# Score matmuls of both heads of a pair in one alternating group, later chunks spread over the expert slots, and a planner that may keep an engine free

## The chip, the cores and the metric

The kernel runs on one core of a Trainium2 chip. A core has a matmul engine (TensorE, PE in the profile, with its weight loads as PEld), VectorE (DVE), ScalarE (ACT), GpSimd (POOL) and SyncE (SP), which here issues nearly all DMAs. The metric is device microseconds for one execution. An execution of the kernel before takes 314.53 us (median of three runs, 313.73 to 315.22).

## The reference, cut to what matters

Stage one is a linear attention with a decaying state, for 4 batches, 8 heads, 768 steps and head size 48. Stage two sends each of the 3072 rows of its result (384 wide) through four two-layer experts and adds them with row weights.

```python
for t in range(S):                       # per batch and head
    cur = outer(u * k[t], v[t])
    y[t] = r[t] @ (state + cur)
    state = w[:, None] * state + outer(k[t], v[t])
x = y.transpose(0, 2, 1, 3).reshape(3072, 384)
p = domain_probs / (domain_probs.sum(-1) + 1e-9)
for e in range(4):                       # w1: 384 x 1024, w2: 1024 x 384
    out += p[:, e:e+1] * (relu(x @ w1[e]) @ w2[e])
```

## The kernel before, in words

**Tiles.** The 768 steps are cut into 6 pieces of 128 for each of the 4 batches: 24 chunks, `ci` = 0 to 23, batch `ci % 4`, piece `ci // 4`. Four chunks with the same piece form a group of 512 rows, `sc` = 0 to 5, which the experts take at once.

**One chunk of attention.** Three loads bring R, K and V (`Rt`, `Kt`, `Vt`, line 172, 192 KB each). DVE multiplies R and K with powers of the decay (`RK`, line 287; jobs `scale`). `RK` is turned so that the head size lies along partitions (`RKT`): for chunks 0 to 9 by PE transposes (line 337) and a copy, from chunk 10 on by a DMA transpose that SP issues (line 326). Two heads share the 128 partitions: the first of each pair has rows 0 to 63, the second rows 64 to 127. The score matmuls (`At_ps`, line 357) contract over 64 rows only: four for the first heads (`j` = 0), into one PSUM tile, and four for the second heads (`j` = 1), into another. In the program these are two jobs, `("At", ci, 0)` and `("At", ci, 1)`, that the planner may put apart. DVE masks each tile (`AtM`, line 366); PE multiplies with V and with the old state (`Y_ps`, lines 381 and 388); DVE adds the current step's share (`Ysb`, line 397), for which POOL and DVE make `ruk`, `dcoef` and `dv`. `Ysb` is transposed into the experts' input `xTe` (by PE to chunk 9, by DMA from chunk 10). For the state, PE makes `St_ps` (line 429), DVE adds it to the old state (`Tn`, line 444), and POOL scales it into `S` (line 449), which the same batch's next chunk reads four chunks later.

**The experts.** `SLOTS` lists 24 pairs of an expert `e` and a group `sc`, in the order of their rank. A slot is 8 first-layer groups (`hT_ps`, line 490: 3 matmuls of 512 columns; for three early slots line 484: 12 matmuls of 128 columns, chunk by chunk), each followed by an ACT relu, and 4 second-layer groups (`out_ps`, line 515: 8 matmuls of 384 columns), each followed by an evacuation into `oacc` (line 523 on ACT for expert 0, line 525 on DVE for the others). The weights arrive in 24 pieces (`wst`, lines 180 and 183), and ACT or DVE casts each to bf16 (lines 72 and 74).

**What sets the order.** Every piece of work is a job with a cost per engine, needed jobs, buffers that it takes and a rank. A small event-driven planner (lines 547 to 632) runs at build time: whenever an engine is free, it takes the job of least rank that is ready and whose buffers are free. The sequence it finds is what is issued, engine by engine; on the chip each engine works through its own sequence in that order, and waits only for the data and buffers of the instruction that is next. Attention jobs have ranks below those of most expert jobs, so attention runs as early as its loads allow, and SP's order of loads is `ORDER` (line 191). Where the planner expects PE to idle in the first 30 us, it puts in matmuls on constants (`spin`, line 157).

Of the kernel before, what the change touches and what calls it, by code (L numbers as in the profile page):

```python
# [19 lines left out]
def kernel(  # L20
# [12 lines left out]
    nc = tc.nc  # L33
# [96 lines left out]
    BACKLOG = 6.0  # L130
    SLOTS = [(0, 0, 1), (1, 0, 0), (0, 1, 1), (1, 1, 1), (2, 0, 0), (2, 1, 0), (3, 0, 0), (3, 1, 0)]
# [9 lines left out]
    def job(name, on, run, needs=(), rank=0.0, takes=(), drops=(), moves=None):  # L141
        j = Job()
        j.name, j.on, j.run, j.needs, j.rank = name, on, run, list(needs), rank
# [22 lines left out]
    def load_chunk(ci):  # L166
        b, c = ci % B, ci // B
        sl = slice(c * C, (c + 1) * C)
        for i, (n, src) in enumerate((("Rt", r), ("Kt", k), ("Vt", v))):
            def run(n=n, src=src):  # L170
                t = tl[n, ci] = work.tile([128, H, D], F32, tag=n, bufs=NIN, name=n)
                nc.sync.dma_start(t, src[b, :, sl, :].transpose([1, 0, 2]))
            load_job((n, ci), 1.0, run, (("inp", ci),))

    def load_w(m, e):
        for i, (a, bb) in enumerate(PIECES):
            def run(i=i, a=a, bb=bb):
                t = tl["wst", m, e, i] = work.tile([128, 3 * Dm], F32, tag="wst", bufs=8, name="wst")
                if m == 1:
                    nc.sync.dma_start(t[:, 0:(bb - a) * Dm].rearrange("p (d f) -> p d f", d=NDB),  # L180
                                      w1_v[e][:, :, a * 128:bb * 128])
                else:
                    nc.sync.dma_start(t[:, 0:(bb - a) * Dm].rearrange("p (f d) -> p f d", d=Dm),
                                      w2_v[e][:, a:bb, :])
            load_job(("wst", m, e, i), 0.52 * (bb - a), run, (("wst", m, e, i),))
# [5 lines left out]
    ORDER = ("c0 p w1e0 c1 c2 c3 w2e0 c4 w1e1 w2e1 c5 c6 c7 w1e2 w2e2 c8 w1e3 c9 w2e3 " +  # L191
             " ".join(f"c{i}" for i in range(10, TOTC))).split()
    for what in ORDER:
        if what == "p":
            load_p()
        elif what[0] == "c":
            load_chunk(int(what[1:]))
        else:
            load_w(int(what[1]), int(what[3:]))


    def cast(m, e, i, rank):
# [11 lines left out]
        if e == 0:  # L214
            on = {"A": 0.36 * n}
        job(("cast", m, e, i), on, run, [("wst", m, e, i)], rank, (), (("wst", m, e, i),))
# [51 lines left out]
    job("pn", {"V": 1.1}, c_pn, ["pt"], 5.5, (), (("mm", "pp"),))  # L268
# [7 lines left out]
    def attention(ci):  # L276
# [6 lines left out]
        pre = [("S", ci - NRK), ("T", ci - NRK, 1)] if ci >= NRK else []  # L283

# [46 lines left out]
        else:  # L331
# [21 lines left out]
        def at(j):  # L353
            def run():
                ps = tl["At", ci, j] = psum.tile([128, NP, C], F32, tag="At", bufs=2, name="At_ps")
                for q in range(NP):
                    nc.tensor.matmul(ps[:, q, :], tl["RKT", ci][j * P2:(j + 1) * P2, 1, q, :],  # L357
                                     tl["RKT", ci][j * P2:(j + 1) * P2, 0, q, :],
                                     start=True, stop=True)
            return run  # L360

        def mk(j):
# [316 lines left out]
```

## Time and profile before

| | us |
|---|---|
| median of the timed runs | 314.53 |
| the profiled execution, whole | 316.11 |
| its span in the trace | 314.3 |
| PE busy | 299.6 (95%) |
| DVE busy | 161.6 (51%) |
| ACT busy | 155.2 (49%) |
| POOL busy | 102.3 (33%) |

How to read it: the span runs from the first instruction of the program to its last, and the profiled execution took 1.8 us more than its span. PE's busy time counts each matmul from its start to its modelled end, and matmuls overlap, so a PE that shows as busy can still be waiting for up to the length of a matmul; what a matmul costs in a stream is read from the starts of the ones that follow. The timeline view merges equal instructions that follow one another: start, time from the first start to the last end, line, operation, count, and in brackets the idle time before and what ended it.

### The profile page before, as it was taken

To read this page: it belongs to the slowest core of one execution; us is meant where nothing else is said; L and a number is where in the kernel's file an instruction comes from. 1 tells how busy PE (TensorE), PEld (TensorE's weight loads), DVE (VectorE), ACT (ScalarE), POOL (GpSimd) and SP (SyncE) were. 2 spreads that over 40 slices of the span, in tenths; PEclk is the share of its full clock that TensorE was granted. 3 is DMA by queue.
4 is the path that set the end of the run, shared out by engine and by line. 5 is a ranking of instruction groups with operands and counts; after the bars stand their busy time and mean duration, and the time that the engine had idled before them with its cause. 6 is when DMAs were issued, how large, how long until landed. Compare 5 with 4: busy or idle time off the path is not lost.

```text
span 314.3 us, 5691 instructions
## 1 busy us (share of the span) xinstructions
PE 299.6 (95%) x2232; PEld 172.3 (55%) x2232; DVE 161.6 (51%) x298; ACT 155.2 (49%) x253; POOL 102.3 (33%) x133
## 2 busy tenths in 40 slices
PE   5799999999998999998999999999999999999995
PEld 2476566876554555555555555555555555555553
DVE  5797578988989997697732231022210221201223
ACT  5467867756333333333545345734456444465440
POOL 3375097566999984756400000000000000000000
PEclk9999999999999999999999999999999999999999
DMA  7999999999999995799500031000020000200002
GB/s 166 250 268 259 298 187 366 255 255 215 206 197 174 177 194 117 190 143 200 118 0 1 2 100 52 1 0 0 27 75 0 2 0 2 75 25 0 2 0 100
DMA packets 108110, 36.92 MB, mean 117 GB/s; under 512 B 96282, under 2 KB 108060, under 8 KB 108084
## 3 DMA queue, kind: packets, MB, share of 16 engines
q1 hardware_dynamic: 108068, 36.56, 49.5%
q8 instruction: 17, 0.28, 0.4%
q14 instruction: 9, 0.07, 0.1%
q10 hardware_dynamic: 16, 0.00, 0.0%
HBM read 26.79 MB, written 4.72 MB: 100 GB/s over the span
## 4 chain that ended last, share of the span: by engine, by line
PE 65%; DMA 16%; DVE 11%; ACT 2%; issue 2%; SPq 2%; POOL 1%; DVEq 0%; POOLq 0%; ACTq 0%
PE out_ps L515 31%; PE hT_ps L490 29%; DMA wst<-in_moe_w_dram 8%; DVE RK L287 4%; DMA RKT<-RK 3%; DVE AtM L366 3%; DMA Rt<-in_r_dram 2%; DMA Kt<-in_k_dram 2%; PE At_ps L357 2%; PE hT_ps L484 2%; DVE oacc L525 1%; DVE Tn L444 1%; ACT hTs L499 1%; DVE Ysb L397 1%; PE RKT_ps L337 1%
## 5 line engine op out<-in xcount | busy, mean ns | idle before, releaser
L501 ACT ACTIVATE hTs<-hT_ps 128x512 bf16<-128x512 f32 x168 | 99.8, 597 | 113.2 <-PE hT_ps L490 108.8
L515 PE MATMUL out_ps<-w_sb,hTs 128*128 128x384 bf16 x768 | 139.9, 326 | 0.0
L490 PE MATMUL hT_ps<-xTe,w_sb 128*128 128x512 bf16 x504 | 124.3, 379 | 0.0
L525 DVE SCALAR_TENSOR_TENSOR oacc<-out_ps,p_nat,oacc 128x384 f32<-128x384 f32 x72 | 44.3, 616 | 124.1 <-PE out_ps L515 123.9
L515 PEld LDWEIGHTS <-hTs 128*128 128x128 bf16 x768 | 73.9, 98 | 54.9
L490 PEld LDWEIGHTS <-w_sb 128*128 128x128 bf16 x504 | 46.8, 98 | 46.9
L366 DVE TENSOR_TENSOR AtM<-At_ps,mask 128x512 bf16<-128x512 f32 x48 | 32.5, 684 | 3.2 <-PE At_ps L357 2.9
L299 POOL TENSOR_TENSOR ruk<-Rt,Kt 128x384 f32<-128x384 f32 x24 | 25.1, 1050 | 20.9 <-DMA Kt<-in_k_dram 20.8
L303 POOL TENSOR_TENSOR ruk<-ruk,U_sd 128x384 f32<-128x384 f32 x24 | 26.6, 1107 | 1.5 <-ACT U_sd L244 1.0
L319 POOL TENSOR_TENSOR dv<-Vt,dcoef 128x384 f32<-128x384 f32 x24 | 21.2, 885 | 14.4 <-DVE Ysb L397 8.2
L449 POOL TENSOR_TENSOR S<-Tn,wC 64x192 bf16<-64x192 f32 x32 | 18.5, 579 | 13.6 <-DVE Tn L444 12.2
L523 ACT ACTIVATE oacc<-out_ps,p_nat 128x384 f32<-128x384 f32 x24 | 13.9, 580 | 17.7 <-PE out_ps L515 17.7
L357 PE MATMUL At_ps<-RKT 64*128 64x128 bf16 x192 | 18.7, 222 | 2.8 <-DMA RKT<-RK 1.1
L72 ACT CAST w_sb<-wst 128x1152 bf16<-128x1152 f32 (+1 forms) x16 | 16.3, 1032 | 8.1 <-DMA wst<-in_moe_w_dram 8.1
L484 PE MATMUL hT_ps<-xTe,w_sb 128*128 128x128 bf16 x288 | 19.4, 223 | 0.4 <-DVE xTe L74 0.4
L287 DVE TENSOR_TENSOR RK<-Rt,W_sd 128x384 bf16<-128x384 f32 x20 | 17.4, 870 | 2.1 <-DMA Rt<-in_r_dram 2.1
L357 PEld LDWEIGHTS <-RKT 64*128 64x128 bf16 x192 | 10.6, 95 | 14.2 <-issue 7.4
L484 PEld LDWEIGHTS <-w_sb 128*128 128x128 bf16 x288 | 17.1, 100 | 1.4 <-DVE xTe L74 0.5
L287 DVE TENSOR_TENSOR RK<-Kt,W_sd 128x384 bf16<-128x384 f32 x20 | 17.2, 859 | 0.6 <-DMA Kt<-in_k_dram 0.5
L314 DVE TENSOR_REDUCE dcoef<-ruk 128x8 f32<-128x384 f32 x24 | 13.0, 546 | 6.5 <-POOL ruk L303 6.3
L499 ACT ACTIVATE hTs<-hT_ps 128x512 bf16<-128x512 f32 x24 | 13.6, 600 | 3.0 <-PE hT_ps L484 2.8
L397 DVE TENSOR_TENSOR Ysb<-Y_ps,dv 128x384 bf16<-128x384 f32 x24 | 13.2, 549 | 1.3 <-PE Y_ps L388 1.2
(59 smaller groups left out, 134.8 us busy)
## 6 DMA issues: line engine op xcount, KB each, us to landing
wst<-in_moe_w_dram SPq DMA_DIRECT2D x16, 576.0 KB, 5.7
Rt<-in_r_dram SPq DMA_DIRECT2D x24, 192.0 KB, 3.8
Kt<-in_k_dram SPq DMA_DIRECT2D x24, 192.0 KB, 4.0
Vt<-in_v_dram SPq DMA_DIRECT2D x24, 192.0 KB, 3.9
out_dram<-oacc SPq DMA_DIRECT2D x24, 192.0 KB, 2.1
wst<-in_moe_w_dram SPq DMA_DIRECT2D x8, 384.0 KB, 6.4
RKT<-RK SPq DMA_TRANSPOSE x14, 3.8
xTe<-Ysb SPq DMA_TRANSPOSE x14, 2.5
```

Source lines behind the costliest of these rows:

```text
L287: nc.vector.tensor_mul(RK[:, i, :, 0:D], tl[("Kt", "Rt")[1 - i], ci], tl["W", i] if ci < SUB else W_sd[i])
L299: nc.gpsimd.tensor_mul(tl["ruk", ci], tl["Rt", ci], tl["Kt", ci])
L303: lambda: nc.gpsimd.tensor_mul(tl["ruk", ci], tl["ruk", ci], U_sd),
L319: nc.gpsimd.tensor_mul(tl["dv", ci], tl["Vt", ci], tl["dcoef", ci].to_broadcast((128, H, D)))
L357: nc.tensor.matmul(ps[:, q, :], tl["RKT", ci][j * P2:(j + 1) * P2, 1, q, :], tl["RKT", ci][j * P2:(j + 1) * P2, 0, q, :], start=True, stop ...
L366: nc.vector.tensor_mul(tl["AtM", ci][:, j], tl["At", ci, j], mask[:, None, :].to_broadcast((128, NP, C)))
L449: nc.gpsimd.tensor_mul(S_new[pr, :, cl], tl["Tn", ci][pr], wC[pr, :, None].to_broadcast((P2, NP, D)))
L484: nc.tensor.matmul(ps[:, i, :], w1_sb[:, e, db, (fb + i) * 128:(fb + i + 1) * 128], xTe[:, db, s0, :], start=(i == 0 and db == 0), stop=(i ...
L490: nc.tensor.matmul(ps[:, 0:n, :].rearrange("p a b -> p (a b)"), w1_sb[:, e, db, fb * 128:(fb + 1) * 128], xTe[:, db, s0:s0 + n, :].rearran ...
L501: nc.scalar.activation(hTs[:, fb, s0:s0 + n, :], ps[:, 0:n, :], AF.Relu)
L515: nc.tensor.matmul(ps, tl["hTs", e, sc][:, fb, s, :], w2_sb[:, e, fb, :], start=(fb == 0), stop=(fb == NFB - 1))
L525: nc.vector.scalar_tensor_tensor(tl["oacc", ci], in0=tl["o", e, ci], scalar=pe, in1=tl["oacc", ci], op0=ALU.mult, op1=ALU.add)
```

## The change

The change has these parts, all in how jobs are defined and planned; what is computed is the same.

1. The two score jobs of a chunk become one, whose eight matmuls alternate between the first and the second head of each pair. Both masks need that one job.
2. The scale jobs of chunks 8 to 23 need the first first-layer group of the slot that stands `LEAD` = 5 places earlier in `SLOTS` (chunk 12: slot 7). This is a need in the planner; on the chip it shows only in the order of each engine's instructions.
3. A job may stand `behind` another: it may start on its engine as soon as the other has been issued, not only when it has ended (second transpose, second mask).
4. In the first 30 us of the plan, an engine that could start a job is kept free if a job of lower rank will be ready for it within 0.6 of the first job's cost.
5. At the start of the kernel: chunk 1's R and K are loaded between the pieces of expert 0's first weights, the row probabilities after chunk 3; the state of the first four chunks and the normalised probabilities wait until the fourth chunk's output is out; POOL may cast expert 0's second weights.

```diff
+    HURRY = 30.0
+    LEAD = 5
...
-    ORDER = ("c0 p w1e0 c1 c2 c3 w2e0 c4 w1e1 w2e1 c5 c6 c7 w1e2 w2e2 c8 w1e3 c9 w2e3 " +
+    ORDER = ("c0 w1e0.0 R1 K1 w1e0.1 w1e0.2 V1 c2 c3 p w2e0 c4 w1e1 w2e1 c5 c6 c7 w1e2 w2e2 c8 w1e3 c9 w2e3 " +
...
         if e == 0:
             on = {"A": 0.36 * n}
+            if m == 2:
+                on["P"] = 0.45 * n
...
-    job("pn", {"V": 1.1}, c_pn, ["pt"], 5.5, (), (("mm", "pp"),))
+    job("pn", {"V": 1.1}, c_pn, ["pt", ("Yout", SUB - 1)], 3.0, (), (("mm", "pp"),))
...
         pre = [("S", ci - NRK), ("T", ci - NRK, 1)] if ci >= NRK else []
+        if ci >= 2 * SUB:
+
+            e_g, sc_g, one = SLOTS[ci - LEAD]
+            pre.append(("l1", e_g, sc_g, 0, 0))
...
-                    [("scale", ci, i)] + ([("T", ci, 0)] if i else []), on_pe,
-                    (("tr", "T", ci),) if i == 0 else ())
+                    [("scale", ci, i)], on_pe, (("tr", "T", ci),) if i == 0 else (),
+                    behind=(("T", ci, 0),) if i else ())
...
-        def at(j):
-            def run():
-                ps = tl["At", ci, j] = psum.tile([128, NP, C], F32, tag="At", bufs=2, name="At_ps")
-                for q in range(NP):
-                    nc.tensor.matmul(ps[:, q, :], tl["RKT", ci][j * P2:(j + 1) * P2, 1, q, :],
+        def at():
+
+            for j in range(2):
+                tl["At", ci, j] = psum.tile([128, NP, C], F32, tag="At", bufs=2, name="At_ps")
+            for q in range(NP):
+                for j in range(2):
+                    nc.tensor.matmul(tl["At", ci, j][:, q, :],
+                                     tl["RKT", ci][j * P2:(j + 1) * P2, 1, q, :],
                                      tl["RKT", ci][j * P2:(j + 1) * P2, 0, q, :],
                                      start=True, stop=True)
-            return run
...
+        job(("At", ci), {"T": 0.42}, at, [ready], on_pe, (("At", ci, 0), ("At", ci, 1)), (("RKT", ci),))
         for j in range(2):
-            job(("At", ci, j), {"T": 0.23}, at(j), [ready] + ([("At", ci, 0)] if j else []), on_pe,
-                (("At", ci, j),), (("RKT", ci),))
-            job(("mask", ci, j), {"V": 0.61}, mk(j), [("At", ci, j)] + ([("mask", ci, 0)] if j else []),
-                rk - 0.5, (("AtM", ci),) if j == 0 else (), (("At", ci, j),))
+            job(("mask", ci, j), {"V": 0.61}, mk(j), [("At", ci)],
+                rk - 0.5, (("AtM", ci),) if j == 0 else (), (("At", ci, j),),
+                behind=(("mask", ci, 0),) if j else ())
...
-        job(("Sm", ci), {"T": 0.17}, smm, [("Y", ci), "wC"] + ([("S", ci - B)] if c else []), on_pe + 1,
+        job(("Sm", ci), {"T": 0.17}, smm, [("Y", ci), "wC", ("S", ci - B) if c else ("Y", SUB - 1)], on_pe + 1,
...
+    def fits(j):
+        if any(n not in gone for n in j.behind):
+            return False
+        new = [t[0] for t in j.takes if t not in held]
+        return all(free[n] >= new.count(n) for n in new)
...
+        if got is not None and now < HURRY:
+
+            us = got.on[e]
+            for i in soon[e]:
+                if i.name not in gone and i.rank < got.rank and fits(i) and                         now < known[i.name] < now + 0.6 * us:
+                    heapq.heappush(waiting[e], (got.rank, got.no, got))
+                    heapq.heappush(events, (known[i.name], seq, "eng", e))
+                    seq += 1
+                    return False
```

Three places show how the instructions move. The lines of the changed kernel stand 18 to 20 further down: its 377 is line 357 before, 510 is 490, 535 is 515, 305 is 287, 386 is 366, 464 is 444.

PE, the score matmuls of chunk 12. Before, the eight matmuls of `RKT_1562` (left out here after the first of each four):

```order
L388 MATMUL Y_ps_1697<-Vb_1500,AtM_1645 128x48
L357 LDWEIGHTS RKT_1562
L357 MATMUL At_ps_1713<-RKT_1562 128x128
...
L490 LDWEIGHTS w1_sb_70
L490 MATMUL hT_ps_1718<-xTe_720,w1_sb_70 128x512
...
L357 MATMUL At_ps_1726<-RKT_1562 128x128
...
L429 LDWEIGHTS RK2_105
```

and after the change, those of `RKT_1881`:

```order
L510 MATMUL hT_ps_1910<-xTe_734,w1_sb_70 128x512
L377 LDWEIGHTS RKT_1881
L377 MATMUL At_ps_1916<-RKT_1881 128x128
...
L377 MATMUL At_ps_1917<-RKT_1881 128x128
...
L535 LDWEIGHTS hTs_1729
L535 MATMUL out_ps_1927<-w2_sb_71,hTs_1729 128x384
```

Two groups of four with other work between them, each for one PSUM tile, have become one group of eight in which every second matmul is for the other tile and the other half of the rows.

DVE, the masks of chunk 9, the last whose operand PE transposes; `S_0_111` is the state of chunk 8's batch, the casts are of expert 3's second weights. Before:

```order
L397 TENSOR_TENSOR Ysb<-Y_ps,dv 128x384
L74 CAST w_sb<-wst 128x1152
L444 TENSOR_TENSOR Tn<-S_0_111,St_ps 64x192 x2
L314 TENSOR_REDUCE dcoef<-ruk 128x8
L74 CAST w_sb<-wst 128x1152
L74 COPY xTe<-xT_ps 128x3x128
L366 TENSOR_TENSOR AtM<-At_ps,mask 128x512
L287 TENSOR_TENSOR RK_105<-Rt,W_sd 128x8x48
L366 TENSOR_TENSOR AtM<-At_ps,mask 128x512
```

and after:

```order
L417 TENSOR_TENSOR Ysb<-Y_ps,dv 128x384
L74 CAST w_sb<-wst 128x1152
L464 TENSOR_TENSOR Tn<-S_0_111,St_ps 64x192 x2
L74 COPY xTe<-xT_ps 128x3x128
L386 TENSOR_TENSOR AtM<-At_ps,mask 128x512 x2
```

One of the two casts has moved to ACT, and chunk 10's first scale no longer stands between the masks.

DVE, the scales of chunk 11 (`RK3_106`) and its masks. Before:

```order
L287 TENSOR_TENSOR RK3_106<-Rt_1318,W0_sd_127 128x8x48
L525 SCALAR_TENSOR_TENSOR oacc_1035<-out_ps_1438,p_nat_131,oacc_1035 128x384
L397 TENSOR_TENSOR Ysb_1484<-Y_ps_1456,dv_1388 128x384
L314 TENSOR_REDUCE dcoef_1497<-ruk_1434 128x8
L287 TENSOR_TENSOR RK3_106<-Kt_1323,W1_sd_128 128x8x48
...
L366 TENSOR_TENSOR AtM_1645<-At_ps_1626,mask_92 128x512
```

and after:

```order
L464 TENSOR_TENSOR Tn_1714<-S2_0_115,St_ps_1702 64x192 x2
L305 TENSOR_TENSOR RK3_106<-Rt_1330,W0_sd_127 128x8x48
L305 TENSOR_TENSOR RK3_106<-Kt_1340,W1_sd_128 128x8x48
L545 SCALAR_TENSOR_TENSOR oacc_1027<-out_ps_1731,p_nat_131,oacc_1027 128x384
L545 SCALAR_TENSOR_TENSOR oacc_1238<-out_ps_1749,p_nat_131,oacc_1238 128x384
L386 TENSOR_TENSOR AtM_1795<-At_ps_1775,mask_92 128x512
```

The scales now follow directly on the state sum of the chunk before, and only two evacuations stand between them and the masks that need their product; before there were 14 rows of other work. From chunk 10 on this pattern repeats once per slot. On PE, between the state matmuls of one chunk (line 449) and the score matmuls of the next, stand six first-layer groups and two second-layer groups; on SP, one DMA transpose of `RK` per slot, with the loads of a chunk four places later behind it.

More of the change, by code (lines that the diff above doesn't have):

```diff
@@ L139, with job @@
         pass
-    def job(name, on, run, needs=(), rank=0.0, takes=(), drops=(), moves=None):
+    def job(name, on, run, needs=(), rank=0.0, takes=(), drops=(), moves=None,
+            behind=()):
         j = Job()
+        j.behind = behind
         j.name, j.on, j.run, j.needs, j.rank = name, on, run, list(needs), rank
@@ L561 @@
     gone = set()
+    unknown = {n: len(q) for n, q in left.items()}
+    known = {n: 0.0 for n in left}
+    soon = {e: [] for e in avail}
     held = set()
@@ L583, in start @@
             if ready_at[j.name] <= now + 1e-9 and \
-                    all(t in held or free[t[0]] > 0 for t in j.takes) and \
+                    fits(j) and \
                     not (j.moves and e == "S" and dma_free[0] > now + BACKLOG):
@@ L607, in start @@
         heapq.heappush(events, (end, seq + 1, "done", j))
+        for u2 in users.get(j.name, ()):
+            unknown[u2.name] -= 1
+            known[u2.name] = max(known[u2.name], end)
+            if not unknown[u2.name] and end < HURRY + 5:
+                for e2 in u2.on:
+                    soon[e2].append(u2)
         seq += 2
```

45 lines of the change are left out of this document (25 added, 20 removed).

## The prediction

> **What bounds the kernel now.** I read the windows view first, over stretches cut where its character changes (columns: stretch, length, busy us and instructions of PE, its weight loads, DVE, ACT and POOL, granted clock, DMA share, GB/s).
>
> ```profile
> 0.00:30.00 30.00, 23.16 (x234) 15.71 (x235) 22.59 (x60) 18.44 (x29) 14.84 (x24) 1.00 0.92 229
> 30.00:77.00 47.00, 45.11 (x526) 32.43 (x524) 37.44 (x64) 32.62 (x50) 26.50 (x33) 1.00 1.00 269
> 77.00:160.00 83.00, 80.36 (x653) 44.15 (x650) 71.32 (x125) 29.77 (x50) 60.99 (x77) 1.00 0.86 166
> 160.00:311.00 151.00, 150.94 (x829) 80.02 (x826) 29.70 (x50) 74.33 (x125) 0.00 (x0) 1.00 0.07 22
> 311.00:314.30 3.30, 0.00 (x0) 0.00 (x0) 0.60 (x1) 0.00 (x0) 0.00 (x0) 0.84 0.33 119
> ```
>
> Four regimes follow one another. To 30 us everything starts up, PE idles 6.8 us. From 30 to 77 us PE is nearly full, but the DMA engines are full (1.00): work cannot come sooner than its data. From 77 to 160 us DVE (71.3 of 83) and PE share the load and PE idles 2.6 us. From 160 us attention is over and PE alone is busy, without a gap, for 151 us; 3.3 us of evacuation and store end the span. So a microsecond of PE work or PE waiting saved after 77 us is saved at the end; one saved before 77 us counts only if the data were there.
>
> The second view is the PE timeline in the third stretch, for the price of a score group.
>
> ```profile
> 113.66 0.82 PE L490 MATMUL hT_ps<-xTe,w_sb 128*128 128x512 bf16 x3
> 114.32 1.46 PE L515 MATMUL out_ps<-w_sb,hTs 128*128 128x384 bf16 x8
> 115.62 0.33 PE L381 MATMUL Y_ps<-S,RKT 128*128 128x96 bf16 x4
> ...
> 116.14 0.81 PE L490 MATMUL hT_ps<-xTe,w_sb 128*128 128x512 bf16 x3
> 116.88 0.39 PE L357 MATMUL At_ps<-RKT 64*128 64x128 bf16 x4
> 117.20 0.82 PE L490 MATMUL hT_ps<-xTe,w_sb 128*128 128x512 bf16 x3
> ```
>
> From start to start, three matmuls of line 490 take 0.66 us when line 515 follows, and 0.74 when a score group follows: 0.08 is lost on entering. The group itself holds PE for 0.32 us, though its four matmuls step by only (0.39 - 0.22) / 3 = 0.058 us; about 0.09 goes on leaving. One group costs 0.32 + 0.08 = **0.40 us**, a chunk 0.80, and some 0.17 of every 0.40 is the turn into 64-row matmuls and out again.
>
> **The change part by part.** *Pairing (A).* The trace holds one case where both groups of a chunk were queued together, chunk 0:
>
> ```profile
> 9.97 0.62 PE L357 MATMUL At_ps<-RKT 64*128 64x128 bf16 x8 [0.86 <-DVE RKT L74]
> ```
>
> and, of all its score matmuls (duration min/median/max in ns),
>
> ```profile
> L357 PE MATMUL At_ps<-RKT x192: 212/216/311, 10.0 to 159.1; 64*128 64x128 bf16 x192
> ```
>
> Eight in 0.62 us. The array was slow there (0.311 us each, the maximum, against 0.216); even at the fast step of 0.058 eight in sequence would need 7 x 0.058 + 0.31 = 0.72. So the two halves ran side by side. The alternating order of the change makes that the rule: four steps of 0.058, one turn in and out of 0.17, about 0.41 us per chunk in place of 0.80, **0.39 saved**. Chunks 10 to 23 have their score work after 77 us: 14 x 0.39 = **5.5 us**. Lower bound, if nothing runs side by side and one turn is saved: 0.17 a chunk, 2.4 us. Upper bound, 0.45 a chunk (a whole group and some of the turn): 6.3. I take 5.5, by the row of eight.
>
> *PE's idle time after 77 us (B).* Its waits in that stretch (total, times, longest):
>
> ```profile
> PE At_ps L357 <- DMA RKT<-RK: 1.1, 1, 1.1
> PE St_ps L429 <- DVE Tn L444: 0.9, 1, 0.9
> PE At_ps L357 <- DVE AtM L366: 0.3, 1, 0.3
> PE St_ps L429 <- DVE Ysb L397: 0.2, 1, 0.2
> ```
>
> All four are score or state matmuls waiting for a crowded DVE or for its product's transpose. With chunks 10 to 23 paced one per slot (10.4 us of expert work: eight groups of 0.65, four of 1.30), DVE has a fixed load per slot. From the groups of the page (busy us and mean ns of one behind the bar):
>
> ```profile
> L525 DVE SCALAR_TENSOR_TENSOR oacc<-out_ps,p_nat,oacc 128x384 f32<-128x384 f32 x72 | 44.3, 616 | 124.1 <-PE out_ps L515 123.9
> L366 DVE TENSOR_TENSOR AtM<-At_ps,mask 128x512 bf16<-128x512 f32 x48 | 32.5, 684 | 3.2 <-PE At_ps L357 2.9
> L314 DVE TENSOR_REDUCE dcoef<-ruk 128x8 f32<-128x384 f32 x24 | 13.0, 546 | 6.5 <-POOL ruk L303 6.3
> L397 DVE TENSOR_TENSOR Ysb<-Y_ps,dv 128x384 bf16<-128x384 f32 x24 | 13.2, 549 | 1.3 <-PE Y_ps L388 1.2
> L449 POOL TENSOR_TENSOR S<-Tn,wC 64x192 bf16<-64x192 f32 x32 | 18.5, 579 | 13.6 <-DVE Tn L444 12.2 <-POOL S L449 0.3
> ```
>
> Four evacuations 2.46, two masks 1.37, two scales 1.71 (twice the median below), `dcoef` 0.55, `Ysb` 0.55 and a state sum of 0.74 (below) make 7.4 us of some 11; DVE is no longer near its limit. The 2.6 us of idle go, and with each of the four waits up to 0.16 that the modelled end of the last matmul covers (0.216 long, next possible after 0.058): **3.2 us**. Bounds 0 (each returns elsewhere) and 3.2.
>
> *The new wait (C).* The pacing takes away slack: the score group of a chunk now follows its scales closely. In the trace the same chain stands once, spread over PE, DVE, POOL and SP:
>
> ```profile
> 127.85 0.33 PE L429 MATMUL St_ps<-Vb,RK 128*128 128x96 bf16 x4
> 128.02 1.46 PE L515 MATMUL out_ps<-w_sb,hTs 128*128 128x384 bf16 x8
> 128.22 0.74 DVE L444 TENSOR_TENSOR Tn<-S,St_ps 64x192 f32<-64x192 bf16 x2 [0.29 <-PE St_ps L429]
> 128.75 1.28 POOL L449 TENSOR_TENSOR S<-Tn,wC 64x192 bf16<-64x192 f32 x2
> 128.99 0.68 DVE L287 TENSOR_TENSOR RK<-Kt,W_sd 128x384 bf16<-128x384 f32 x1
> 129.70 1.24 SPq L326 DMA_TRANSPOSE RKT<-RK  x1
> ```
>
> State matmuls start at 0; state sum done and scale begun at 1.14; two scales at 0.68 end at 2.50; the transpose is issued at 2.53. If an evacuation (0.62) stands before the state sum, 3.15. The transpose lands 3.1 to 4.9 us after its issue, and a scale takes 0.54 to 1.36 (the views of the tile `RKT` and of line 287):
>
> ```profile
> DMA to landing us min/median/max: 3.1/3.8/4.9
> ```
>
> ```profile
> L287 DVE TENSOR_TENSOR RK<-Rt,W_sd x20: 542/856/1362, 26.5 to 151.1; 128x384 bf16<-128x384 f32 x20
> ```
>
> So the operand is there at 5.6 to 6.3 with the shortest landing, 6.9 with the median one. PE in that time has its state matmuls (127.85 to 128.02, 0.17), six groups of 0.66 and two of 1.30: it asks at 6.7. The slack is 0.4 to 1.1 us, or -0.2. SP's queue before that transpose holds loads four chunks ahead and stores, both long released, and the loads of one chunk per slot (0.59 MB, at the 269 GB/s above 2.2 us of 11) leave the DMA engines mostly idle, so I take the short landing: **0.4 us lost in all**, with 14 x 0.2 = 2.8 as the near bound. If PE does wait, the masks of that chunk and DVE's evacuations behind them start that much later; four PSUM buffers absorb it.
>
> *The front (D).* Load order, deferred states, the planner's held engines, second transposes and masks `behind`, and the pairing of chunks 1 to 9 all act before 77 us. There the work hangs on data: DVE's casts wait for weights, and chunk 9's scale and masks stand behind them.
>
> ```profile
> 65.83 0.95 DVE L74 CAST w_sb<-wst 128x768 bf16<-128x768 f32 x1 [0.73 <-DMA wst<-in_moe_w_dram]
> 66.70 0.68 DVE L366 TENSOR_TENSOR AtM<-At_ps,mask 128x512 bf16<-128x512 f32 x1
> 67.30 1.23 DVE L287 TENSOR_TENSOR RK<-Rt,W_sd 128x384 bf16<-128x384 f32 x1
> ...
> 70.50 0.76 DVE L74 CAST w_sb<-wst 128x1152 bf16<-128x1152 f32 x1 [0.73 <-DMA wst<-in_moe_w_dram]
> ...
> 72.40 0.89 DVE L74 CAST w_sb<-wst 128x1152 bf16<-128x1152 f32 x1
> ...
> 73.84 0.69 DVE L366 TENSOR_TENSOR AtM<-At_ps,mask 128x512 bf16<-128x512 f32 x1
> ...
> 70.51 1.50 PE L484 MATMUL hT_ps<-xTe,w_sb 128*128 128x128 bf16 x24
> 71.85 1.46 PE L515 MATMUL out_ps<-w_sb,hTs 128*128 128x384 bf16 x8
> ...
> 75.50 1.46 PE L515 MATMUL out_ps<-w_sb,hTs 128*128 128x384 bf16 x8
> 76.80 0.33 PE L381 MATMUL Y_ps<-S,RKT 128*128 128x96 bf16 x4
> ```
>
> The bytes and their sequence to this point are the same after the change, so the cast that waited until 70.50 waits until then again, whatever was won before. What moves is one cast of 0.89 to ACT. After the first cast, at 71.2, DVE then has the state sum (0.73), a copy (0.36) and both masks (2 x 0.69), done at 73.7. PE takes chunk 9's product there, with one single-chunk group (half of the 1.34 from 70.51 to 71.85, 0.67) and one second-layer group (1.30) behind it that it had done before that product until now: 75.7 against 76.8. I take **0.8 us** won, between 0 and 1.5, since how soon PE is there is not sure. POOL's two new casts can delay chunk 3's `dv` behind them by a few us at 25 us; that is hidden by the same wait for data, and without it would cost up to 2.
>
> Sum: 5.5 + 3.2 + 0.8 - 0.4 = **9.1 us**. The profiled execution took 316.1 (span 314.3 and 1.8 around it), which gives 307.0; it was 1.6 above the median of the timed runs, so on the median: 314.5 - 9.1 = **305.4 us**.
>
> **The rivals.** *Late operands (slower).* Place: the score group of chunks 10 to 23. With DVE and POOL at the same time the scales take 1.36, and the landing is 4.4: 1.14 + 0.62 + 2.72 + 0.03 + 4.4 = 8.9 against 6.7, 2.2 us late in each of 14 slots, 31 us lost against 9.5 won: 336. It decides from 9.5 / 14 = 0.68 us late per slot, an operand at 7.4. For it: half of the scales took 0.86 or more, and pacing ties every slot to one such chain. Against: those stood beside the long POOL products of other chunks, and landings over 4 us belong to stretches with a full DMA queue. 8%.
>
> *The scale waits out POOL's state update.* By the row at 128.75 that update (0.58 a piece, mean of its group) starts inside every such chain. If a scale had to wait for each piece: 2 x (0.55 + 0.58) = 2.26 in place of 1.36, operand at 7.2, 0.5 late, 14 x 0.5 = 7.0, and the time 312. The row at 128.99 speaks against it: beside that update the scale took 0.68, not 1.13. 7%. The Trainium skill, "SBUF — State Buffer", section "SBUF: two separate sides", states just this rule: a VectorE instruction with two SBUF inputs and a GpSimd instruction take turns on a shared port pair, and the one that comes second waits for the whole of the other. By it the time would be that of this rival; the trace agrees only in the long scales, up to 1.36.
>
> *One turn saved, nothing side by side.* A is 2.4, time 308.5. Against it stands the row of eight. 8%.
>
> *The front passes its gains on.* If data, not its transport, was the limit, 9 x 0.39 = 3.5 of chunks 1 to 9 and the 1.9 us that PE idles from 30 to 77 us come on top: 300 to 302. The DMA share of 1.00 speaks against it. 12%.
>
> *No difference.* The planner's sequence loses at the start what A and B win, over 7 us; the front has 6.8 us of idle to lose in, and it must be lost past the data's own time. 5%.
>
> **How the numbers follow.** Forecast 60% (303.5 to 307.5 with the bounds of C and D); the rivals 8, 7, 8, 12 and 5. No change is within 0.5% or 1.6 us, about what a measurement of this kernel can tell. Faster: 60 + 7 + 8 + 12 = 87%; same 5%; slower 8%. The range from 301.2 to 311.5 leaves out late operands and no difference (13%), half of the port rival and a third of the front's: 2 in 10.
>
> **What would show it.** A: score rows of eight, 0.60 us or less from start to modelled end. B: attention runs to some 250 us, DVE below 75% in every stretch after 80. C: PE's waits for `RKT` by DMA sum to under 1 us; over 9 would make the forecast wrong in sign. D: the same expert work is done on PE at 77 us, within 1.5 us. A score row of eight lasting 0.75, or expert groups 0.2 us longer around it, would refute the pairing.

## The result, and the profile after

The changed kernel takes 305.97 us (median of four runs, 305.80 to 307.27). The kernel before took 314.20 beside it (four runs, 313.73 to 315.22). The ratio is 0.974, 95% interval 0.971 to 0.978: 8.2 us less, where 9.1 less and 305.4 us were forecast. The profiled execution took 306.04 (span 304.3) against 316.11 (span 314.3). Some executions, one of the changed kernel too (307.27 us, mean granted clock 0.994), ran at a lower mean clock, and the ratios leave out the two that stood far above the rest of their kernel, 442.04 of the kernel before and 310.90 of e7.

Its windows, with the same columns as those of before (stretch, length, busy us and instructions of PE, PEld, DVE, ACT, POOL, granted clock, DMA share, GB/s):

```profile
0.00:30.00 30.00, 23.11 (x237) 15.31 (x237) 21.43 (x55) 16.93 (x28) 16.64 (x26) 1.00 0.93 223
30.00:77.00 47.00, 43.91 (x535) 31.76 (x535) 35.45 (x68) 33.69 (x50) 25.45 (x34) 1.00 0.99 272
77.00:160.00 83.00, 83.00 (x567) 44.63 (x565) 46.88 (x84) 38.01 (x64) 39.17 (x52) 1.00 0.56 115
160.00:240.00 80.00, 80.00 (x557) 43.19 (x555) 39.35 (x69) 38.08 (x65) 18.66 (x25) 1.00 0.36 78
240.00:300.80 60.80, 60.80 (x342) 32.46 (x340) 13.60 (x23) 27.94 (x47) 0.00 (x0) 1.00 0.06 22
300.80:304.30 3.50, 0.07 (x1) 0.00 (x0) 0.62 (x1) 0.00 (x0) 0.00 (x0) 1.00 0.31 112
```

From 77 us to its last matmul PE is busy all the time (83.00 of 83, 80.00 of 80, 60.80 of 60.80), and the view of PE's waits is empty there; before, 2.6 us were idle. DVE falls from 71.3 to 46.9 us in the third stretch and carries the rest to 240 us; the last attention matmul ends at 241 us, where some 250 was forecast. Before 77 us PE idles more than before (3.1 us against 1.9 from 30 to 77): the front is as full of waits as it was.

A score group in PE's timeline, paced. `At_ps` is line 377 now, the first layer 510, the second 535:

```profile
157.98 1.46 PE L510 MATMUL hT_ps<-xTe,w_sb 128*128 128x512 bf16 x6
159.37 0.40 PE L377 MATMUL At_ps<-RKT 64*128 64x128 bf16 x8
159.70 1.47 PE L535 MATMUL out_ps<-w_sb,hTs 128*128 128x384 bf16 x8
```

Eight matmuls from start to modelled end take 0.40 us, where four took 0.39. From start to start the group holds PE for 0.33; the six matmuls ahead take 1.39 in place of 6 x 0.216, so entering costs 0.09. A chunk's score work is 0.42 us of PE's time in all. Before, it was 0.80 by the prediction's reading. The starts of single matmuls in the trace of before are finer than that row: entering cost 0.096 there and a group of four held PE for 0.326, which makes 0.84 a chunk.

The transposed operand: the issue for chunk 13 on SP, the PE row that uses it, and from the view of the tile `RKT` (77 to 250 us) the time from issue to landing:

```profile
121.43 1.24 SPq L344 DMA_TRANSPOSE RKT<-RK  x1
```

```profile
125.30 0.40 PE L377 MATMUL At_ps<-RKT 64*128 64x128 bf16 x8
```

```profile
DMA to landing us min/median/max: 3.1/3.1/3.6
```

The operand landed at about 124.5, 0.8 us before PE asked. This slack is 0.24 us for chunk 10, 0.5 to 0.8 for those of chunks 12 to 20 whose landing is on record, 1.7 for chunks 21 and 22 and 3.3 for chunk 23.

### The profile page after: what moved, and what is told of

Read it like the earlier page. It is cut to its first block, busy times and chain, and to the rows that moved or that the text cites. A ratio compares the mean times of both kernels' runs of the same rounds, so it can differ in the third digit from the quotient of the medians.

```text
span 304.3 us, 5693 instructions
## 1 busy us (share of the span) xinstructions
PE 290.9 (96%) x2231; PEld 167.4 (55%) x2231; DVE 157.3 (52%) x296; ACT 154.7 (51%) x253; POOL 99.9 (33%) x135
## 4 chain that ended last, share of the span: by engine, by line
PE 78%; DMA 10%; SPq 5%; DVE 3%; issue 1%; ACT 1%; POOL 0%; DVEq 0%
PE out_ps L535 38%; PE hT_ps L510 34%; DMA wst<-in_moe_w_dram 9%; SPq L178 3%; DMA Kt<-in_k_dram 2%; SPq L187 2%; PE At_ps L377 2%; DVE AtM L386 1%; PE Y_ps L408 1%; PE Y_ps L401 1%; DVE w_sb L74 1%; PE St_ps L449 1%; PE hT_ps L504 1%; ACT w_sb L72 1%; PE RKT_ps L355 0%
## 5 line engine op out<-in xcount | busy, mean ns | idle before, releaser
L510 PEld LDWEIGHTS <-w_sb 128*128 128x128 bf16 x504 | 47.3, 98 | 45.3
L386 DVE TENSOR_TENSOR AtM<-At_ps,mask 128x512 bf16<-128x512 f32 x48 | 31.0, 684 | 25.4 <-PE At_ps L377 25.4
L337 POOL TENSOR_TENSOR dv<-Vt,dcoef 128x384 f32<-128x384 f32 x24 | 20.4, 853 | 16.2 <-DVE Ysb L417 7.8
L321 POOL TENSOR_TENSOR ruk<-ruk,U_sd 128x384 f32<-128x384 f32 x24 | 24.5, 1023 | 2.1 <-ACT U_sd L258 1.0
L72 ACT CAST w_sb<-wst 128x1152 bf16<-128x1152 f32 (+1 forms) x15 | 15.3, 1023 | 13.3 <-DMA wst<-in_moe_w_dram 13.3
L504 PEld LDWEIGHTS <-w_sb 128*128 128x128 bf16 x288 | 17.5, 101 | 3.2 <-issue 1.7
L305 DVE TENSOR_TENSOR RK<-Kt,W_sd 128x384 bf16<-128x384 f32 x20 | 15.1, 753 | 0.4 <-DMA Kt<-in_k_dram 0.3
L305 DVE TENSOR_TENSOR RK<-Rt,W_sd 128x384 bf16<-128x384 f32 x20 | 11.9, 595 | 2.0 <-DMA Rt<-in_r_dram 1.7
L464 DVE TENSOR_TENSOR Tn<-S,St_ps 64x192 f32<-64x192 bf16 x32 | 11.1, 347 | 1.9 <-PE St_ps L449 1.4
L76 POOL CAST Vb<-Vt 128x384 bf16<-128x384 f32 x20 | 10.3, 516 | 2.5 <-PE St_ps L449 2.3
```

The source lines that it names most:

```text
L72: nc.scalar.copy(o, i)
L305: nc.vector.tensor_mul(RK[:, i, :, 0:D], tl[("Kt", "Rt")[1 - i], ci], tl["W", i] if ci < SUB else W_sd[i])
L321: lambda: nc.gpsimd.tensor_mul(tl["ruk", ci], tl["ruk", ci], U_sd),
L337: nc.gpsimd.tensor_mul(tl["dv", ci], tl["Vt", ci], tl["dcoef", ci].to_broadcast((128, H, D)))
L386: nc.vector.tensor_mul(tl["AtM", ci][:, j], tl["At", ci, j], mask[:, None, :].to_broadcast((128, NP, C)))
L504: nc.tensor.matmul(ps[:, i, :], w1_sb[:, e, db, (fb + i) * 128:(fb + i + 1) * 128], xTe[:, db, s0, :], start=(i == 0 and db == 0), stop=(i ...
```

## The experiments

Theory: the sum of the prediction. Pairing (A) takes some 0.4 us a chunk off PE, the pace (B) takes away PE's waits, both after 77 us, where PE sets the end; the front (D) gives little, the new wait (C) almost nothing. Rivals: the parts are worth something else apart; pairing saves a turn only; operands come late. In the notes below, a time is the median of that kernel; the kernel before, run between, had medians of 312.9 to 313.6, so the ratios count.

**e1: pairing alone.**

```diff
-            job(("At", ci, j), {"T": 0.23}, at(j), ...)
+        job(("At", ci), {"T": 0.42}, at, [ready], on_pe, (("At", ci, 0), ("At", ci, 1)), ...)
```

> The kernel before with one edit: the eight score matmuls of a chunk are one job, the two halves in turn, and both masks need that job. Load order, deferred states and the pace stay as they were. Theory (the terms of the prediction add): the score work of a chunk falls from 0.84 to 0.42 us of PE time, 14 chunks after 77 us give 5.7 to 5.9; the waits of PE after 77 us stay near 2.6 us, since DVE is as crowded as before: 308 to 309.5 against 314.2. Rival (the pairing only turns PE work into waiting as long as DVE holds 71 of 83 us from 77 to 160 us): PE waits after 77 us grow by 2 us or more, time 311 or more.

Measured: 315.54 us, ratio 1.006 (1.003 to 1.009). The pairing alone did not make the kernel faster; the rival's numbers came true. PE's waits after 77 us:

```profile
PE At_ps L359 <- DMA RKT<-RK: 4.3, 4, 2.0
PE St_ps L430 <- DVE Ysb L398: 1.1, 2, 0.7
PE out_ps L516 <- DVE oacc L526: 1.0, 1, 1.0
PE hT_ps L491 <- issue: 0.5, 3, 0.2
```

They sum to 6.9 us, 4.4 more than before. The longest, around 126 us, in rows of DVE, SP and PE (times in order):

```profile
118.59 1.33 DVE L287 TENSOR_TENSOR RK<-Kt,W_sd 128x384 bf16<-128x384 f32 x1
...
122.41 0.54 DVE L398 TENSOR_TENSOR Ysb<-Y_ps,dv 128x384 bf16<-128x384 f32 x1
```

```profile
121.63 2.46 SPq L405 DMA_TRANSPOSE xTe<-Ysb  x1
124.18 1.26 SPq L326 DMA_TRANSPOSE RKT<-RK  x1
```

```profile
123.93 1.46 PE L516 MATMUL out_ps<-w_sb,hTs 128*128 128x384 bf16 x8
127.38 0.55 PE L359 MATMUL At_ps<-RKT 64*128 64x128 bf16 x8 [1.98 <-DMA RKT<-RK]
```

The second scale ended at 119.92, but SP issued its transpose at 124.18. Ahead of it in SP's queue stood a transpose of `Ysb`, which DVE finished only at 122.95. So PE stood at the score group until the operand had landed. And the wait had a price of its own, in the windows after it:

```profile
127.00:127.40 0.40, 0.02 (x2) 0.03 (x4) 0.00 (x0) 0.00 (x0) 0.00 (x0) 1.00 0.75 213
127.40:130.80 3.40, 3.18 (x25) 1.79 (x27) 2.62 (x4) 0.60 (x1) 0.83 (x1) 0.51 1.07 211
130.80:131.20 0.40, 0.40 (x7) 0.23 (x5) 0.00 (x0) 0.03 (x1) 0.00 (x0) 0.89 1.17 237
```

For 3.4 us after it the granted clock was 0.51: another 3.4 x 0.49 = 1.7 us. Together 4.4 + 1.7 - 5.9 (14 chunks at 0.42) = 0.2 us more; the two profiled executions differ by 0.6 (316.73 against 316.11). Six of the ten executions, this one among them, have a mean granted clock of 0.995 or less, and a median of 316.1; the four others have 314.0, the kernel before 313.6. So the waits eat what the pairing saves, and most of the loss beyond that goes with the half clock.

**e2: the pace alone.**

```diff
+        if ci >= 2 * SUB:
+            e_g, sc_g, one = SLOTS[ci - 5]
+            pre.append(("l1", e_g, sc_g, 0, 0))
```

> The kernel before with one edit: the scales of chunks 8 to 23 also need the first group of first-layer matmuls of the slot five places earlier. The two halves of a score product stay apart. Theory: PE waits of 2.6 us after 77 us (3.2 with the modelled ends) go and nothing takes their place: 311 to 311.5. Rival (operands come late once attention is paced; with two separate groups there is less expert work between the state matmuls and the scores): waits for RKT of 0.2 us and more a slot, 314 or more.

Measured: 312.76, ratio 0.995 (0.992 to 0.998), 1.5 us less; 2.5 to 3 were expected. No wait of PE is left after 77 us, as expected, so B's gain is there. Part of it is given back earlier: up to 77 us PE idles 10.1 us, against 8.7 in the kernel before. Of the score matmuls, 72 have been done by 77 us (view of the tile `At_ps`), 80 in the kernel before:

```profile
L360 PE MATMUL At_ps<-RKT x72: 216/216/311, 9.7 to 66.1; 64*128 64x128 bf16 x72
```

The gate begins at chunk 8, so one chunk's score work moves past 77 us; that this is why PE idles more before is likely, but not shown. The forecast had put no cost on it.

**e3: pairing and pace, without the front.** Both edits above in the kernel before.

> The kernel before with both edits above, and nothing of the front (load order, deferred states, held engines, the cast on POOL, the masks behind each other). Theory: A and B add, 5.7 and 3.2 less: 305.5 from the median of 314.2 without the front, and the front of the whole change is then worth at most the 0.8 us of the prediction, on either side: 305.3 to 306.8. Rival (the front matters and the parts do not add): 308 or more.

Measured: 305.48, ratio 0.973 (0.970 to 0.975), 8.6 us less, as expected. Against the whole change (0.974, 0.971 to 0.978) no difference can be told: the front's own edits are worth nothing that shows, 0.5 us on the wrong side with about 1.4 either way (the pairing of chunks 1 to 9, which the prediction counts to the front, is in e3 too). The two edits together give 8.6; apart they give -1.9 and 1.5.

**e4: the changed kernel without the pace.**

```diff
-            e_g, sc_g, one = SLOTS[ci - LEAD]
-            pre.append(("l1", e_g, sc_g, 0, 0))
```

> The changed kernel without the pace (the lines that make the scales of chunks 8 to 23 need a slot's first matmuls). Theory: the waits of PE after 77 us come back, 2 to 3 us, the rest stays: 308 to 309 against 306.0, and attention ends before 165 us again. Rival (pairing and the new front had already removed what PE waited for, the pace is worth nothing): 305.7 to 306.7.

Measured: 311.84, ratio 0.995 (0.992 to 0.998); 308 to 309 was expected. Without the pace 6.5 us are lost by the ratios, twice the 3.2 of term B. The window of the crowded stretch, and the waits of PE after 77 us that are over 1 us:

```profile
77.00:160.00 83.00, 77.31 (x654) 43.26 (x663) 68.66 (x126) 32.15 (x54) 60.29 (x77) 1.00 0.84 166
```

```profile
PE At_ps L373 <- DMA RKT<-RK: 2.1, 4, 0.8
PE Y_ps L404 <- DVE AtM L382: 1.8, 4, 0.9
```

All waits sum to 4.8 us. Again PE, with less to do per chunk, waits for attention.

**e5: head after head in one job.**

```diff
-            for q in range(NP):
-                for j in range(2):
+            for j in range(2):
+                for q in range(NP):
```

> The changed kernel with the two loops of the score job exchanged: first the four matmuls of one half, then the four of the other, still one job. Theory (what counts is that both halves are queued together; chunk 0 of the kernel before, written in this order, ran its eight in 0.62 us): as the changed kernel, 305.5 to 306.5, score rows of eight of 0.40 us. Rival (the matmuls run one after another as they are written, only the alternation makes them pairs): seven steps of 0.056 and one turn, 0.64 a chunk in place of 0.42, 14 x 0.22 = 3 us more, 309.

Measured: 306.11, ratio 0.975 (0.970 to 0.981), the same as the changed kernel.

```profile
103.74 0.41 PE L377 MATMUL At_ps<-RKT 64*128 64x128 bf16 x8
```

Being queued together makes the pairs; the alternation adds nothing that can be measured.

**e6: both halves on the same rows.**

```diff
-        tl["RKT", ci][j * P2:(j + 1) * P2, 1, q, :],
-        tl["RKT", ci][j * P2:(j + 1) * P2, 0, q, :],
+        tl["RKT", ci][(0 if dmat else j * P2):(P2 if dmat else (j + 1) * P2), 1, q, :],
+        tl["RKT", ci][(0 if dmat else j * P2):(P2 if dmat else (j + 1) * P2), 0, q, :],
```

> The changed kernel; from chunk 10 on both halves of a score product read rows 0 to 63 of RKT, so that the second half computes the first one's product again and no two can share the array. Theory: eight steps of 0.056 and one turn of 0.19, 0.64 us a chunk in place of 0.42: 14 x 0.22 = 3.1 us more, 309, score rows of 0.61. If only the turn saved had counted (the rival 'one turn saved, nothing side by side'): no difference, 306.

Measured: 308.92, ratio 0.985 (0.981 to 0.989), 3.4 us more than the changed kernel by the ratios; 3.1 were expected.

```profile
103.25 0.62 PE L377 MATMUL At_ps<-RKT 64*128 64x128 bf16 x8
```

0.62 against 0.40 is what running side by side is worth, 0.22 a chunk. The times alone would not prove it, since three of the four executions have a mean granted clock of 0.993 or 0.994, against one of four of the changed kernel. The traces do: behind 77 us both kernels have full clock and no wait of PE, and there the fourteen groups hold PE for 7.7 us from start to start, 4.6 in the changed kernel, 3.1 more. The trace has a PE wait of 2.0 us too, in the front, ending at 67.2 us, and half clock behind it (two of the windows). At 77 us its PE is four state matmuls, two transposes and one expert matmul behind the changed kernel, some 0.5 us by their steps, which with the 3.1 makes the 3.5 us between the two profiled executions.

```profile
68.00:69.00 1.00, 1.00 (x13) 1.00 (x11) 0.19 (x1) 0.00 (x0) 1.00 (x3) 0.50 1.10 370
...
71.00:72.00 1.00, 1.00 (x19) 0.88 (x17) 0.39 (x2) 0.58 (x1) 0.00 (x0) 1.00 1.12 319
```

**e7: the operand half a microsecond later.**

```diff
+                if dmat and i == 1:
+                    for _ in range(1):
+                        nc.vector.tensor_mul(scratch, W_sd[0], U_sd)
                 nc.vector.tensor_mul(RK[:, i, :, 0:D], ...)
```

> The changed kernel with one product more on DVE (128x384, into a tile that nothing reads) between the two scales of chunks 10 to 23, about 0.5 us later for the transpose; the planner does not know of it. In the changed kernel the operand lands 0.5 to 0.8 us before PE asks (0.24 for chunk 10). Theory (term C: slack of 0.4 to 1.1 us covers it): 306 to 306.8, PE waits for RKT under 0.6 us in all. Rival (the slack is not there; every delay counts in each of the 14 slots): 14 x 0.5 = 7 us, 313.

Measured: three executions of 306.13 to 308.63 us, median 306.83, ratio 0.980 (0.976 to 0.985); the fourth, which was the profiled one, took 310.90. By the ratios that is 1.9 us more, give or take 1.9, where at most 0.8 was expected. DVE in one paced chunk of the profiled execution:

```profile
112.01 0.58 DVE L309 TENSOR_TENSOR RK<-Rt,W_sd 128x384 bf16<-128x384 f32 x1
112.51 0.86 DVE L308 TENSOR_TENSOR scratch<-W_sd,U_sd 128x384 bf16<-128x384 f32 x1
113.29 0.55 DVE L309 TENSOR_TENSOR RK<-Kt,W_sd 128x384 bf16<-128x384 f32 x1
```

The scales end 1.83 us after the first began; in the changed kernel 1.36 (rows under e10), so the delay is 0.47. Ten of the fourteen score groups still do not wait. The four waits in PE's timeline are 0.29, 0.34, 0.54 and this one, of chunk 10:

```profile
92.92 0.40 PE L381 MATMUL At_ps<-RKT 64*128 64x128 bf16 x8 [2.06 <-DMA RKT<-RK]
```

So the slack covers half a microsecond in most slots, but not for chunk 10, whose scales here ended 1.9 us later than in the changed kernel and not 0.47: the first began 1.0 us later, and the three products took 2.57 us where the two had taken 1.68. What made DVE start late was not followed up. After that wait the clock fell to 0.50 again, for 3.4 us. The waits (3.2 us in all) and the half clock (1.7) together are the 4.9 us by which this execution is longer than that of the changed kernel; the three others have no trace.

**e8: the operand a microsecond later.** As e7 with `range(2)`.

> As the run before with two such products, about 1.0 us later. Theory (the rival 'late operands' has the right price beyond the slack): 0.35 us late in 13 slots and 0.8 in one, 5 us, 311 (309 to 313), all of it as PE waits for RKT. Rival (PE gets later operands for nothing, its queue or other work fills the gap): under 307.

Measured: 315.74, ratio 1.008 (1.003 to 1.012), 10.4 us more than the changed kernel by the ratios; 309 to 313 was expected. Its profiled execution took 313.27, 7.2 more than that of the changed kernel, and its waits:

```profile
PE At_ps L381 <- DMA RKT<-RK: 7.7, 10, 2.0
```

```profile
109.99 0.58 DVE L309 TENSOR_TENSOR RK<-Rt,W_sd 128x384 bf16<-128x384 f32 x1
110.49 1.45 DVE L308 TENSOR_TENSOR scratch<-W_sd,U_sd 128x384 bf16<-128x384 f32 x2
111.86 0.55 DVE L309 TENSOR_TENSOR RK<-Kt,W_sd 128x384 bf16<-128x384 f32 x1
```

The delay is 2.42 - 1.36 = 1.06; the waits are 0.25 to 1.28, and 2.0 for chunk 10. What goes beyond the slack is lost in full, 7.7 of waits for 7.2 of time, and nothing fills the gap. Chunks 21 to 23, with the long slack, do not wait. The other four executions took 0.5 to 3.7 us longer than the profiled one. Three of them have a mean granted clock of 0.995, so a stretch of half clock as in e1, worth 1.7 us, is likely in them; no trace shows it, or the rest. This is the rival *late operands* made real: 1 us later in each slot costs all that the change won.

**e9: no pace, but the planner told.**

```diff
-        us = 0.48 if ci < SUB else 0.65
+        us = 0.48 if ci < SUB else 0.65 if ci < DMAT else 0.90
-            end = dma_free[0] + 1.0
+            end = dma_free[0] + (2.5 if j.name[0] == "T" else 1.0)
```

(on top of e4's edit)

> The changed kernel without the pace (as e4), but the planner is told dearer scales (0.90 in place of 0.65 us from chunk 10 on) and that a transposed operand lands 1.5 us later than it had reckoned, so that it places score matmuls behind more expert work. Theory now (without the pace PE stands at score matmuls because they were put into its queue before their operand can be there, not because DVE has too little time in all): PE waits for RKT after 77 us fall from 2.1 to under 0.7 us, time 307 to 309 against 311.8 in e4. Rival (DVE, busy 69 of 83 us, is the bound there; whatever the order, PE waits for it somewhere): waits move to masks and evacuations, 311 or more.

Measured: 309.00, ratio 0.987 (0.981 to 0.992); 307 to 309 was expected. PE's waits after 77 us:

```profile
PE At_ps L373 <- DMA RKT<-RK: 2.2, 2, 1.5
PE Y_ps L397 <- DVE Tn L460: 0.3, 1, 0.3
```

They fell from 4.8 to 2.5 us though DVE is as busy in that stretch as in e4 (69.2 of 83 us). By the ratios 2.7 of the 6.5 us that the missing pace costs came back, so some two fifths were a wrong place in PE's queue, not a lack of DVE time. The waits for `RKT` did not fall as expected (2.2, two long ones); those for masks went. The profiled execution (309.40) is still 3.4 us longer than that of the changed kernel, and the 2.5 us of waits that are left are most of it. Whether a better order would remove them too, or only a lighter DVE, no run shows.

**e10: POOL's state update cut to one column.**

```diff
+                n = 1 if ci >= DMAT - B else D
+                cl = slice(j * D, j * D + n)
-                nc.gpsimd.tensor_mul(S_new[pr, :, cl], tl["Tn", ci][pr], ...)
+                nc.gpsimd.tensor_mul(S_new[pr, :, cl], tl["Tn", ci][pr][:, :, 0:n], ...)
```

> The changed kernel; the state update on POOL of chunks 6 and later works on one column of each head's 48 (the rest of the state is not updated). Theory (a scale on DVE that starts beside a piece of that update only moves on once the piece has ended, 0.28 us on the second scale, and this lies under the slack of 0.6 us before PE asks): both scales take 0.55 to 0.60 us in paced chunks in place of 0.58 and 0.86, the operand lands 0.25 us earlier, and the time stays at 305.5 to 306.5. Rival (0.86 comes from what the second scale reads or writes, not from POOL): the second scale still takes 0.86.

Measured: 305.13, ratio 0.974 (0.967 to 0.980), no difference, as expected. First the changed kernel, POOL and DVE in one paced chunk (the two pieces of the update, the two scales):

```profile
108.34 0.50 POOL L469 TENSOR_TENSOR S<-Tn,wC 64x192 bf16<-64x192 f32 x1 [0.25 <-DVE Tn L464]
```

```profile
108.92 0.71 POOL L469 TENSOR_TENSOR S<-Tn,wC 64x192 bf16<-64x192 f32 x1
```

```profile
108.68 0.58 DVE L305 TENSOR_TENSOR RK<-Rt,W_sd 128x384 bf16<-128x384 f32 x1
109.18 0.86 DVE L305 TENSOR_TENSOR RK<-Kt,W_sd 128x384 bf16<-128x384 f32 x1
```

Add start and time: POOL's first piece ends at 108.84, the first scale at 109.26, POOL's second piece at 109.63, the second scale at 110.04. Each ends 0.37 to 0.42 us after the end of the one before it on the other engine: they take turns. Now the small update:

```profile
107.98 0.21 POOL L471 TENSOR_TENSOR S<-Tn,wC 64x4 bf16<-64x4 f32 x1 [0.25 <-DVE Tn L464]
```

```profile
108.43 0.52 POOL L471 TENSOR_TENSOR S<-Tn,wC 64x4 bf16<-64x4 f32 x1 [0.25 <-DVE Tn L464]
```

```profile
108.32 0.56 DVE L305 TENSOR_TENSOR RK<-Rt,W_sd 128x384 bf16<-128x384 f32 x1
108.79 0.55 DVE L305 TENSOR_TENSOR RK<-Kt,W_sd 128x384 bf16<-128x384 f32 x1
```

The scales take 0.56 and 0.55, and the second small piece, started while the first scale ran, takes 0.52 where the first took 0.21: it ends at 108.95, 0.07 after the scale's end at 108.88. So the 0.86 was a wait for POOL, 0.3 us of it, and it lies under the slack. Over all fourteen chunks the two scales fell from 1.41 to 1.18 us on average, 0.24 a chunk. The Trainium skill, "SBUF — State Buffer", section "SBUF: two separate sides", says that such instructions of VectorE and GpSimd hold a shared port pair for the whole instruction and the later one waits; these rows agree.

**e11 and e12: no engine held.**

```diff
-    HURRY = 30.0
+    HURRY = 0.0
```

> The changed kernel with the planner's holding of an engine for a job of lesser rank switched off (HURRY = 0), nothing else. Theory (before 77 us the work hangs on data, term D): within 0.8 us of the changed kernel, 305.3 to 306.8. Rival (the held engines carry part of the gain): 307.5 or more.

> The same kernel as the run before (HURRY = 0), with more timed runs, since it came out lowest of all and might beat the changed kernel. If the held engines cost something, its ratio to the kernel before stays at 0.971 with the whole interval below the changed kernel's 0.9743; if they are worth nothing either way, the ratio comes out between 0.971 and 0.975 and the two cannot be told apart.

Measured: 304.38, ratio 0.971 (0.964 to 0.978), and with more runs 304.49, ratio 0.973 (0.969 to 0.977). The first is below the 305.3 to 306.8 that was expected, but the kernel before, run beside it, was lower too (312.88). By the ratios it cannot be told from the changed kernel, nor from e3: holding engines is worth nothing that shows.

## Why the prediction was right, and where it was not

**The time.** 305.97 against 305.4, in the likeliest case and its own range. By the profiled executions 10.1 us went, 9.1 were forecast. The terms as measured below make 9.2 us (5.9 for A, 2.6 for B, 0.7 for D, nothing for C), and 9.8 if the waits that the modelled ends hide were the 0.6 of the forecast; A was 0.4 too small, C 0.4 too dear.

**A, pairing.** Right in mechanism, and in size but for the price of before: 0.42 us a chunk where 0.41 was forecast, against 0.84 and not 0.80, so 14 x 0.42 = 5.9 us of PE's time in place of 5.5. Side by side is shown by e6: 3.1 us of PE's time are lost once the halves share their rows. That kernel is the rival *one turn saved* made real, and at 308.92 us it takes what the rival said (308.5); the changed kernel does not. The reading of chunk 0's row of eight was right too: written head after head, it still paired (e5).

**B, the idle time of PE.** All of the 2.6 us that the trace shows went, as forecast. The 0.6 us more that modelled ends were to hide cannot be told from the rest of the sum.

**What A and B rest on.** The step that failed is the sentence "a microsecond of PE work or PE waiting saved after 77 us is saved at the end". It holds in full only for the two edits together. From 77 to 160 us in the kernel before, PE with less work of its own stands at score groups whose operand is not there; pairing alone turned 5.9 us saved into 4.4 of new waits and 1.7 at half clock (e1). The idle 2.6 us of 83 that the prediction read as the pace's whole worth understated it: paired and unpaced, the loss is 6.5 (e4) or, without the front, 10.1 (315.54 against 305.48). The sum came out because both edits were in the change, and that is luck: nothing in the prediction asked for it. What the pace gives to A is in part order: the planner lays out each of these kernels anew, and e9 got 2.7 us back by a later place for the score groups alone, with DVE as busy as without the pace. How much DVE's lighter load, which B named, gives beside that was not separated.

**C, the new wait.** 0.4 us forecast, none found. The slack was 0.5 to 0.8 in most slots (forecast 0.4 to 1.1), with the shortest landing, 3.1, as chosen. e7 and e8 show that the slack is real and what is behind it: half a microsecond is mostly covered, one costs 7 us and more. The price that *late operands* gave, every microsecond past the slack in each slot, was right; the 2.2 us late that it needed did not come, since the scales took 1.36 together and not 2.72, and the operand landed after 3.1 us and not 4.4.

**D, the front.** 0.8 forecast (0 to 1.5), some 0.7 found. Up to 77 us PE has done nearly the same expert work as before (288 first-layer matmuls of 128 columns both times, 28 of 512 against 27, 104 second-layer ones both times) and 13 small attention matmuls more; by their steps that is the 0.7. None of it can be put down to the front's own edits, which are not told from 0 (e3; the held engines alone e11 and e12). Pairing took some 0.4 us off each of chunks 1 to 9, and PE idled 1.2 us more up to 77 us than before: the rival *the front passes its gains on* fell as well.

**The rival on POOL's update** had the right mechanism and the wrong price. The row at 128.99 (0.68 us), which the prediction held against it, proves little: half of the update's first piece was over when that scale began, and it ended 0.42 us after that piece, as the scales under e10 do, so its 0.68 contains the rest of the wait. The turns cost 0.2 to 0.3 us a chunk, not 0.9, and they were already in the 1.36 us for two scales that the sum used.

## What to carry to other kernels

Where engines work through fixed queues, price an edit that takes work off the busiest engine together with what its next instruction needs: less work in front of a wait is a longer wait, and two edits that are worth 1.5 us and less than nothing apart were worth 8.6 us together here. Test parts alone before putting a number on each. When a chain of operations is tied to every slot, measure its slack by lengthening it; here 0.6 us lay between no wait and a wait in most slots.

## What had not been expected of the hardware

Matmuls of the two row halves ran in pairs whichever way they were written: single starts in the trace of e5 (chunks 10 to 23) stand 12 to 14 ns apart within a pair and 41 to 55 between pairs, in the changed kernel 2 to 4 and 52 to 64. In e6, with both halves on the same rows, all steps are 55 to 68.

After a PE wait of 2 us the granted clock halved for 3.4 us, in e1 (1.98), e6 (2.0) and e7 (2.06); in e8 a wait of 2.00 was not followed by it, and in the kernel before, whose longest wait after 77 us is 1.1, it did not happen. The traces show what set e8 apart. Within each of these traces the clock on record changes only at times a whole number of 3.41 us apart (32, 15 and 23 of them from its first entry to the fall in e1, e6 and e7). Cut at these times, e7 has its wait inside one stretch, while in e8 it lies across two:

```profile
90.71:94.12 3.41, 1.35 (x15) 0.78 (x15) 1.85 (x4) 0.72 (x2) 0.68 (x1) 1.00 0.97 185
94.12:97.54 3.42, 3.42 (x21) 1.72 (x20) 1.54 (x3) 0.60 (x1) 2.00 (x2) 0.50 0.36 70
```

```profile
86.77:90.18 3.41, 3.21 (x17) 1.47 (x15) 3.05 (x5) 1.36 (x3) 2.48 (x3) 1.00 0.07 14
90.19:93.60 3.41, 1.61 (x16) 1.02 (x17) 1.44 (x3) 0.42 (x1) 0.00 (x0) 1.00 1.03 193
93.60:97.01 3.41, 3.41 (x34) 2.04 (x32) 2.05 (x5) 1.20 (x2) 2.81 (x4) 1.00 0.35 72
```

PE idled 2.06 us of the first stretch of e7, and the next ran at half clock; in e1 and e6 it was 1.98 and 2.00. In e8 the larger share is 1.80, and the clock stayed. In the fourteen traces no other stretch between 20 us and the last matmuls holds as much idle time of PE, and no other is followed by half clock. So in these cases a pause counted by how much of it fell into one stretch, with the limit somewhere between 1.8 and 1.98 us, and a wait of 2 us cost either 2 us or 3.7. The Trainium skill, "TensorE: Matmul & The Clock Gate", section "Part 1: The HAM clock gate (the 'warmup' mystery)", gives half clock after an idle window of about 3.4 us, and a window that runs free of the kernel: the length of the stretches and their independence of the wait agree, the 2 us of waiting that were enough are less than it states.
